# K and G with 512-column products and a transposed 128-column remainder, with 1/den and the reloads of x moved

## Chip, core and metric

The kernel runs on one core of a Trainium2 chip. The metric is device time in microseconds of one execution; the kernel before took 207.70 us in the median of three runs (207.67 to 207.72). TensorE is PE, its weight loads PEld, VectorE DVE, ScalarE ACT, GpSimd POOL, SyncE SP.

## The reference

x has S = 2048 tokens of D = 640. It is normalised (xn), and a linear attention with 32 heads of 20 channels and a gelu MLP with F = 1536 hidden channels both start from xn; everything is bf16.

```python
xn = _layernorm(x)
# attention
q, k, v = xn @ wqkv                       # split by 32 heads of 20 channels
phi = lambda t: where(t > 0, t + 1, exp(t)) + 1e-6
kv  = einsum("bhsd,bhse->bhde", phi(k), v);  z = sum_s phi(k)
o   = (phi(q) @ kv) / (phi(q) . z + 1e-6)
# MLP
h   = gelu(xn @ w1 + b1)
out = x + o @ wo + h @ w2 + b2
```

## The kernel before

Tokens lie in NT = 16 tiles of 128, or NC = 4 chunks of 512; D is DT = 5 blocks of 128. A small planner records every instruction for each engine in the order of the Python code; an engine runs its list in that order, and the planner adds a semaphore wait where an instruction reads or overwrites what another engine or a DMA handles. So the order of the code is the order of each queue, SP's DMA queue and ACT's (which also issues DMAs) included, and an instruction that waits holds all that is behind it on its engine. PSUM is eight banks of 512 fp32 columns, handed out in a ring by take(n).

The stages, in PE's order:

1. Load and layernorm. xn is kept by token (xn_tm) and transposed (xnT, by PE for three tiles, by 13 DMA transposes on SP for the rest, L261). The MLP's first product fills the same time (h_unit, L391, gelu on ACT, L395).
2. K, L500: for each token tile, 5 contraction blocks times two halves of 320 columns, 160 matmuls into a pair of banks. phi (L488 to L491) turns each pair into PK: an exponential on ACT (L488), a min/add on DVE (L489), a max/add on DVE that reads PSUM (L491). PK lies where x was, by token.
3. G = xn^T phi(K), L525 (g_group): the attention's kv is (Wv^T G) per head, so V is never formed. For each of 5 blocks f of xn's channels, 16 token tiles times two halves of 320 columns, 160 matmuls; ACT copies each result to GTb (L529). Beside it DVE adds the 16 tiles of PK in fp32 into zsum (L534, L537) and splits the sum in two bf16 parts, zhl (L540, L543); zsum and zhl lie in the memory of Msb, which is filled later. POOL reorders the columns of Wq (L519).
4. Q in four chunks, L566 (q_chunk), transposed, 512 columns, with the same phi. After chunk 0 come z_step (L549) and kvt_step (L576): the products Wv x G for eight groups of four heads, in two halves u = 0 and u = 1, masked by DVE (L583) and packed by POOL.
5. The output. PE begins the MLP's second product of token tile 0 (out_mm, L696), then the denominators of all tokens (den_mm, L630) and M = blockdiag(kv) Wo (m_step, L620), in the order j = 0, 1, 4, 2, 3. Each half of M is copied from PSUM to Msb: half 0 by ACT (L602), half 1 by DVE (L605). After the third j, m_step calls den_eps (L636), and after the last one den_rec takes the reciprocal (L640). ACT's queue issues 12 DMAs (spread, three for each chunk) that spread 1/den over the partitions into rsp, and scale_pq (L645) multiplies a chunk of PQ by it.
6. Each output tile takes 12 matmuls of the MLP and 5 of the attention (PQ and Msb) of 512 columns. The last 128 columns of chunks 0 to 2 are made transposed (rem_mm, L707), closed by rem_done (L712) and put back by a DMA transpose on SP. main_done (L720) adds x plus b2 and ACT's queue stores the tile; two slots of out_sb are used in turn. Chunk 3 has 640 columns by tile, and tile 15 ends in three pieces (L775).

After Q, SP reloads x: x_again(c) for the four chunks into the memory of xnT, then the last 128 columns of chunks 0 to 2 as xrem into the memory of PK, then three DMA transposes of xrem to xrT, of which rem_done(c) reads one.

Of the kernel before, what the change touches and what calls it, by code (L numbers as in the profile page):

```python
# [7 lines left out]
P = 128  # L8
# [104 lines left out]
def bass_parallel_sum__linear_attn_block__dense_activation_gelu__prompt_kernel(  # L113
# [4 lines left out]
    NT = S // P  # L118
# [22 lines left out]
    with contextlib.ExitStack() as es:  # L141
# [22 lines left out]
        Msb = Mf[:].rearrange("p (k d) -> p k d", k=DT)  # L164
        zsum = Mf[:, 0:2 * D].bitcast(FP32)
        zhl = Mf[:, 2 * D:4 * D].rearrange("p (a d) -> p a d", a=2)
        b1tmp = sb("b1tmp", [JT, P], BF16)
# [38 lines left out]
        def bank(b, lo=0, hi=512):  # L206
            return ps[:, b * 512 + lo: b * 512 + hi]
# [25 lines left out]
        r_PQ = [[R_("PQ%d_%d" % (c, j)) for j in range(DT)] for c in range(NC)]  # L233
        r_HG = [[R_("HG%d_%d" % (t, j)) for j in range(JT)] for t in range(NT)]
        r_GT = [R_("GT%d" % f) for f in range(DT)]
        r_KVT = [R_("KVT%d" % w) for w in range(2)]
# [257 lines left out]

        for t in range(NT):
            b = take(2)
            fns = []
            for k in range(DT):
                for h in range(2):
                    fns.append(lambda e, k=k, h=h, b=b, t=t: e.matmul(  # L500
                        bank(b + h, 0, HW), xnT[:, k, t * P:(t + 1) * P],
                        Wqkv[:, k, D + h * HW:D + (h + 1) * HW], start=(k == 0), stop=(k == DT - 1)))
            Pl.ins(pe, fns, reads=r_xnT[t] + [r_Wk], writes=B_[b:b + 2])
            phi(pair(b), b, 2, PK[:, t, :], r_PK[t], r_x[t])

# [15 lines left out]

        def g_group(f):
            b = take(2)
            for i, t in enumerate(tord):
                Pl.ins(pe, [(lambda e, t=t, h=h, b=b, f=f, i=i: e.matmul(  # L525
                    bank(b + h, 0, HW), xn_tm[:, t, f * P:(f + 1) * P],
                    PK[:, t, h * HW:(h + 1) * HW], start=(i == 0), stop=(i == NT - 1))) for h in range(2)],
                    reads=r_xn[t] + [r_PK[t]], writes=B_[b:b + 2])
            Pl.ins(s_, lambda e, b=b, f=f: e.activation(halves(GTb[:, f, :]), pair(b), ACT.Copy),  # L529
                   reads=B_[b:b + 2], writes=[r_GT[f]] + r_W1)  # L530

        def z_sums():
            a, c = tord[0], tord[1]
            Pl.ins(v, lambda e: e.tensor_tensor(out=zsum, in0=PK[:, a, :], in1=PK[:, c, :], op=ALU.add),  # L534
                   reads=[r_PK[a], r_PK[c]], writes=[r_zsum])
            for t in tord[2:]:
                Pl.ins(v, lambda e, t=t: e.tensor_tensor(out=zsum, in0=zsum, in1=PK[:, t, :], op=ALU.add),  # L537
                       reads=[r_PK[t], r_zsum], writes=[r_zsum])
            for i in range(DT):
                Pl.ins(v, lambda e, i=i: e.tensor_copy(plain(zhl[:, 0, :], i), parts(zsum, i)),  # L540
                       reads=[r_zsum], writes=[r_zhl])
            for i in range(DT):
                Pl.ins(v, lambda e, i=i: e.tensor_tensor(out=plain(zhl[:, 1, :], i), in0=parts(zsum, i),  # L543
                                                         in1=plain(zhl[:, 0, :], i), op=ALU.subtract),
                       reads=[r_zsum, r_zhl], writes=[r_zhl])
# [13 lines left out]
        for f in range(DT):  # L559
            g_group(f)  # L560

        def q_chunk(c):
# [9 lines left out]
        def kvt_step():  # L572
            for u in range(2):
# [5 lines left out]
                    for w in ws for k in range(DT)],  # L579
                    reads=[r_Wv] + r_GT, writes=[B_[b]])  # L580
                for lo, hi, i in ((0, 4, 0),) if u == 0 else ((0, 3, 0), (3, 4, 1)):
# [17 lines left out]
        def m_copy(j, b, h):  # L599
            cols = slice(h * HW, (h + 1) * HW)  # L600
            if h == 0:
                Pl.ins(s_, lambda e: e.activation(Msb[:, j, cols], bank(b + h, 0, HW), ACT.Copy),  # L602
# [5 lines left out]
        def m_step(js, bs, after):  # L608
            for n, (j, b) in enumerate(zip(js, bs)):
                for h in range(2):  # L610
# [13 lines left out]
                    m_copy(j, b, h)  # L624
                if n == 2:
                    after()
# [30 lines left out]

        def x_again(c):
            w = MW if c < NC - 1 else D
            dma("sync", x_res[:, c * CH:(c + 1) * CH, 0:w],  # L660
                xv[c * CW:(c + 1) * CW, 0:w].rearrange("(t p) d -> p t d", p=P), [r_xr[c]] + (sum(r_xnT, []) if c == 0 else []))

# [10 lines left out]
        q_chunk(3)  # L673
        for c in range(NC):
            x_again(c)
        dma("sync", xrem.rearrange("p (t d) -> p t d", t=NT - CH),
            xv[0:(NT - CH) * P, MW:D].rearrange("(t p) d -> p t d", p=P), [r_xrem] + r_PK)
        for c in range(NC - 1):
            dma_t("sync", xrT[:, c * CW:(c + 1) * CW].rearrange("p (t q) -> p t q", t=CH),
                  xrem[:, c * CW:(c + 1) * CW], [r_xrT[c]], reads=[r_xrem])  # L680
        Pl.ins(v, lambda e: e.tensor_copy(b2c[:], b2t[:]), reads=[r_b2t], writes=[r_b2c])
# [55 lines left out]
        for c in range(NC):  # L737
            spread(c)
        scale_pq(0)
        for t in range(1, CH):  # L740
# [77 lines left out]
```

## Time and profile before

| | |
|---|---|
| median of three runs | 207.70 us |
| profiled execution | 207.16 us, of which the span of instructions is 205.10 us |
| PE busy | 200.5 us, 98% of the span |
| DVE, ACT, POOL busy | 109.4, 71.3, 35.2 us |
| granted PE clock | 1.0 in the whole span |
| stage K (59.6 to 81.35 us) | PE 21.75 us of 21.75 |
| stage G (81.35 to 103.1) | PE 21.73 of 21.75, DVE 17.15 |
| stage Q with z and kvt (103.1 to 126.35) | PE 23.11 of 23.25, DVE 19.23 |
| denominators and M (128.94 to 131.95) | PE 2.85 of 3.01 |

The stages are stretches of the trace, cut where PE goes from one line to the next. A matmul's record shows its start exactly and its end by a model, and successive records overlap: 160 records of 299 ns lie in 21.73 us. So what a matmul costs in a stream is the stretch divided by the count, and not the mean of the records. A few records are missing: where a chain piece says x49 for 50 matmuls, its time is still that of 50. The median of the runs is 0.54 us above the profiled execution.

### The profile page before, as it was taken

The numbers are of one execution on the slowest core, as the hardware profiler recorded it, in microseconds if no ns is written. First come the engines' busy times: TensorE is split into PE (matmuls) and PEld (weight loads), VectorE is DVE, ScalarE is ACT, GpSimd is POOL, SyncE is SP. The second block draws the span as 40 slices with busy tenths as digits, with TensorE's granted clock in tenths as the row PEclk, the third lists the DMA queues.
The fourth block names the chain that finished last, engine by engine and source line by source line (L and its number), as shares of the span: only waits on it lengthen the run. The fifth ranks groups of instructions, "written<-read, shape, count | busy, mean of one in ns | idle before, by whom it ended". The sixth has DMA issues, their size and how long they took to land.

```text
span 205.1 us, 3575 instructions
## 1 busy us (share of the span) xinstructions
PE 200.5 (98%) x1375; PEld 120.1 (59%) x1386; DVE 109.4 (53%) x231; ACT 71.3 (35%) x133; POOL 35.2 (17%) x85
## 2 busy tenths in 40 slices
PE   7899999999999999999999999999999999999995
PEld 3898757544457777777746444544444444447774
DVE  3784388100007888999348889564629323513322
ACT  2788777666676555111153554300000000000000
POOL 3342156700000000999100200000000000000000
PEclk9999999999999999999999999999999999999999
DMA  5968746797940000000000000979935111102011
GB/s 148 350 177 123 212 118 126 84 373 258 371 138 0 0 0 3 0 0 3 0 0 3 2 0 9 341 180 165 180 81 152 38 41 51 54 26 51 32 40 59
DMA packets 31386, 20.46 MB, mean 100 GB/s; under 512 B 16521, under 2 KB 31369, under 8 KB 31369
## 3 DMA queue, kind: packets, MB, share of 16 engines
q1 hardware_dynamic: 27888, 17.08, 30.7%
q10 hardware_dynamic: 3480, 3.15, 6.9%
q8 instruction: 11, 0.18, 0.4%
q14 instruction: 7, 0.05, 0.1%
HBM read 13.11 MB, written 2.62 MB: 77 GB/s over the span
## 4 chain that ended last, share of the span: by engine, by line
PE 95%; DVE 1%; DMA 1%; ACT 1%; issue 1%; DVEq 0%
PE ps L696 30%; PE ps L391 25%; PE ps L525 11%; PE ps L500 11%; PE ps L566 10%; PE ps L707 5%; DMA xPK<-in_A_x_dram 1%; DVE stats L342 1%; ACT Msb L602 1%; PE ps L576 1%; PE ps L630 1%; PE ps L329 0%; DVE xn_tm L364 0%; DVE W L775 0%; PE ps L372 0%
## 5 line engine op out<-in xcount | busy, mean ns | idle before, releaser
L391 PE MATMUL ps<-xnT,W 128*128 128x128 bf16 (+3 forms) x402 | 52.6, 292 | 0.2
L696 PE MATMUL ps<-W,HG 128*128 128x512 bf16 (+3 forms) x249 | 46.4, 338 | 0.3 <-ACT Msb L602 0.2
L391 PEld LDWEIGHTS ps<-xnT,W 128*128 128x128 bf16 x405 | 33.8, 98 | 18.3 <-issue 0.2
L395 ACT ACTIVATE HG<-ps,b1c 128x128 bf16<-128x128 f32 (+3 forms) x81 | 39.1, 515 | 14.4 <-PE ps L391 13.3
L696 PEld LDWEIGHTS ps<-W,HG 128*128 128x128 bf16 x252 | 24.0, 98 | 20.4 <-ACT Msb L602 0.2
L488 ACT ACTIVATE ek<-ps 128x512 bf16<-128x512 f32 (+1 forms) x36 | 23.2, 645 | 20.4 <-PE ps L566 10.3
L489 DVE TENSOR_SCALAR ek<-ek 128x512 bf16<-128x512 bf16 (+1 forms) x36 | 11.0, 305 | 32.4 <-ACT ek L488 31.3
L500 PE MATMUL ps<-Wqkv,xnT 128*128 128x320 bf16 x160 | 21.9, 299 | 0.0
L525 PE MATMUL ps<-xPK,xn_tm 128*128 128x320 bf16 x160 | 21.9, 299 | 0.0
L566 PE MATMUL ps<-xnT,Wqkv 128*128 128x512 bf16 x97 | 21.4, 379 | 0.2
L696 PE MATMUL ps<-Msb,PQ 128*128 128x512 bf16 (+3 forms) x104 | 20.8, 338 | 0.1
L500 PEld LDWEIGHTS ps<-Wqkv,xnT 128*128 128x128 bf16 x160 | 15.7, 98 | 6.2
L525 PEld LDWEIGHTS ps<-xPK,xn_tm 128*128 128x128 bf16 x160 | 15.7, 98 | 6.1
L519 POOL COPY Wqkv<-Wqkv 128x128 bf16<-128x128 bf16 x25 | 15.1, 603 | 22.9 <-PE ps L500 21.4
L342 DVE BATCH_NORM_STATS2 stats<-xPK 128x6 f32<-128x320 bf16 x32 | 14.0, 477 | 9.1 <-DMA xPK<-in_A_x_dram 9.1
L720 DVE TENSOR_TENSOR W<-ps,xnT 128x512 bf16<-128x512 f32 x12 | 8.3, 691 | 18.2 <-PE ps L696 12.6
L566 PEld LDWEIGHTS ps<-xnT,Wqkv 128*128 128x128 bf16 x100 | 9.7, 98 | 11.4
L696 PEld LDWEIGHTS ps<-Msb,PQ 128*128 128x128 bf16 x105 | 10.1, 98 | 8.4
L491 DVE SCALAR_TENSOR_TENSOR PQ<-ps,ek 128x512 bf16<-128x512 f32 x20 | 13.8, 691 | 2.1
L491 DVE SCALAR_TENSOR_TENSOR xPK<-ps,ek 128x640 bf16<-128x640 f32 x16 | 13.2, 824 | 1.7
L537 DVE TENSOR_TENSOR Msb<-Msb,xPK 128x640 f32<-128x640 f32 x14 | 11.6, 825 | 0.5
L352 POOL TENSOR_TENSOR rstd<-aggr,mhalf 128x1 f32<-128x1 f32 x16 | 9.9, 621 | 8.9 <-DVE aggr L350 8.9
(64 smaller groups left out, 98.0 us busy)
## 6 DMA issues: line engine op xcount, KB each, us to landing
Wqkv<-in_A_wqkv_dram SPq DMA_DIRECT2D x3, 800.0 KB, 6.8
W<-in_B_w_dram SPq DMA_DIRECT2D x4, 480.0 KB, 5.9
W<-in_B_w_dram SPq DMA_DIRECT2D x1, 1920.0 KB, 12.7
xnT<-in_A_x_dram SPq DMA_DIRECT2D x3, 512.0 KB, 4.8
xn_tm<-rden ACTq DMA_DIRECT2D x12, 128.0 KB, 4.2
out_dram<-W ACTq DMA_DIRECT2D x12, 128.0 KB, 1.7
xPK<-in_A_x_dram SPq DMA_DIRECT2D x4, 320.0 KB, 5.3
Wo<-in_A_wo_dram SPq DMA_DIRECT2D x8, 160.0 KB, 8.3
```

The source lines that it names most:

```text
L342: Pl.ins(v, lambda e: e.bn_stats(stats[:, s, 6 * h:6 * h + 6], x_in[:, t, h * HW:(h + 1) * HW]), reads=r_x[t], writes=[r_stats[s][h]])
L391: Pl.ins(pe, [(lambda e, k=k: e.matmul(bank(b, 0, w), W1[:, k, jb * P:(jb + 1) * P], xnT[:, k, tok], start=(k == 0), stop=(k == DT - 1))) ...
L395: Pl.ins(s_, lambda e: e.activation(HG[:, jb, tok], bank(b, 0, w), ACT.Gelu_apprx_tanh, bias=b1c[:, jb:jb + 1]), reads=[B_[b], r_b1c], wri ...
L488: Pl.ins(s_, lambda e: e.activation(e2, src, ACT.Exp), reads=br, writes=[r_ek[s]])
L489: Pl.ins(v, lambda e: e.tensor_scalar(et, et, 1.0, 1e-6, ALU.min, ALU.add), reads=[r_ek[s]], writes=[r_ek[s]])
L491: Pl.ins(v, lambda e: e.scalar_tensor_tensor(out=d2, in0=src, scalar=0.0, in1=e2, op0=ALU.max, op1=ALU.add), reads=br + [r_ek[s]], writes= ...
L500: fns.append(lambda e, k=k, h=h, b=b, t=t: e.matmul(bank(b + h, 0, HW), xnT[:, k, t * P:(t + 1) * P], Wqkv[:, k, D + h * HW:D + (h + 1) * ...
L519: Pl.ins(g, lambda e, k=k, i=i: e.tensor_copy(plain(Wqkv[:, k, D:2 * D], i), parts(Wqkv[:, k, 0:D], i)), reads=[r_Wq], writes=[r_Wk, r_WqP])
L525: Pl.ins(pe, [(lambda e, t=t, h=h, b=b, f=f, i=i: e.matmul(bank(b + h, 0, HW), xn_tm[:, t, f * P:(f + 1) * P], PK[:, t, h * HW:(h + 1) * H ...
L537: Pl.ins(v, lambda e, t=t: e.tensor_tensor(out=zsum, in0=zsum, in1=PK[:, t, :], op=ALU.add), reads=[r_PK[t], r_zsum], writes=[r_zsum])
L566: Pl.ins(pe, [(lambda e, k=k, j=j, b=b: e.matmul(bank(b), Wqkv[:, k, D + j * P:D + (j + 1) * P], xnT[:, k, cc], start=(k == 0), stop=(k == ...
L696: Pl.ins(pe, [(lambda e, i=i, x=x, bk=bk: e.matmul(bank(bk, 0, x[1] - x[0]), seq[i][0], seq[i][1][:, x[0]:x[1]], start=(i == 0), stop=(i = ...
```

## The change

K is made of two products in each chunk: columns 0 to 511 by token tile, one bank and five matmuls of N = 512 a tile; columns 512 to 639 transposed, five matmuls with 128 columns of Wk as the stationary operand and 512 tokens of xnT as the moving one. Its phi goes to PKT (in the memory of Msb), and a DMA transpose on SP puts it back into PK's last 128 columns. G likewise: g_group covers columns 0 to 511, and the new g_rem makes the last 128 columns of all five blocks transposed (PK as stationary operand, xn_tm as moving one, 512 and 128 columns in turn); ACT copies them to GrT and a DMA transpose on SP puts them into GTb. z_sums waits for these transposes, and kvt_step's half u = 1 for that of G.

In m_step the copies of half 1 for j = 4, 2, 3 go from DVE to ACT, and den_eps is called after the second j. x_again of chunk 0 stays where it was; those of chunks 1 to 3, xrem and its transposes come after spread in the code, and the first of them waits for the three spread DMAs of chunk 0.

```diff
@@ -163,6 +163,8 @@
         Mf = sb("Msb", [P, DT * D], BF16)
         Msb = Mf[:].rearrange("p (k d) -> p k d", k=DT)
         zsum = Mf[:, 0:2 * D].bitcast(FP32)
+        PKT = Mf[:, 0:NC * CW]
+        GrT = Mf[:, 4 * D:5 * D]
         zhl = Mf[:, 2 * D:4 * D].rearrange("p (a d) -> p a d", a=2)
         b1tmp = sb("b1tmp", [JT, P], BF16)
         b1c = sb("b1c", [P, JT], FP32)
@@ -232,6 +234,9 @@
         r_PK = [R_("PK%d" % t) for t in range(NT)]
         r_PQ = [[R_("PQ%d_%d" % (c, j)) for j in range(DT)] for c in range(NC)]
         r_HG = [[R_("HG%d_%d" % (t, j)) for j in range(JT)] for t in range(NT)]
+        r_PKT = [R_("PKT%d" % c) for c in range(NC)]
+        r_PKr = [R_("PKr%d" % c) for c in range(NC)]
+        r_GrT, r_GTr = R_("GrT"), R_("GTr")
         r_GT = [R_("GT%d" % f) for f in range(DT)]
         r_KVT = [R_("KVT%d" % w) for w in range(2)]
         r_KVP = [R_("KVP%d" % i) for i in range(3)]
@@ -492,16 +497,24 @@
                                                        op0=ALU.max, op1=ALU.add),
                    reads=br + [r_ek[s]], writes=[res_dst] + extra_w)
 
-        for t in range(NT):
-            b = take(2)
-            fns = []
-            for k in range(DT):
-                for h in range(2):
-                    fns.append(lambda e, k=k, h=h, b=b, t=t: e.matmul(
-                        bank(b + h, 0, HW), xnT[:, k, t * P:(t + 1) * P],
-                        Wqkv[:, k, D + h * HW:D + (h + 1) * HW], start=(k == 0), stop=(k == DT - 1)))
-            Pl.ins(pe, fns, reads=r_xnT[t] + [r_Wk], writes=B_[b:b + 2])
-            phi(pair(b), b, 2, PK[:, t, :], r_PK[t], r_x[t])
+        for c in range(NC):
+            ts = range(c * CH, c * CH + CH)
+            cc = slice(c * CW, (c + 1) * CW)
+            for t in ts:
+                b = take(1)
+                Pl.ins(pe, [(lambda e, k=k, b=b, t=t: e.matmul(
+                    bank(b), xnT[:, k, t * P:(t + 1) * P], Wqkv[:, k, D:D + MW],
+                    start=(k == 0), stop=(k == DT - 1))) for k in range(DT)],
+                    reads=r_xnT[t] + [r_Wk], writes=[B_[b]])
+                phi(bank(b), b, 1, PK[:, t, 0:MW], r_PK[t], r_x[t])
+            b = take(1)
+            Pl.ins(pe, [(lambda e, k=k, b=b, cc=cc: e.matmul(
+                bank(b), Wqkv[:, k, D + MW:2 * D], xnT[:, k, cc],
+                start=(k == 0), stop=(k == DT - 1))) for k in range(DT)],
+                reads=sum((r_xnT[t] for t in ts), []) + [r_Wk], writes=[B_[b]])
+            phi(bank(b), b, 1, PKT[:, cc], r_PKT[c], [])
+            dma_t("sync", PK[:, c * CH:(c + 1) * CH, MW:D], PKT[:, cc], [r_PKr[c]] + sum((r_x[t] for t in ts), []),
+                  reads=[r_PKT[c]])
 
         tord = list(range(NT))
         def parts(ap, i):
@@ -520,22 +533,33 @@
                        reads=[r_Wq], writes=[r_Wk, r_WqP])
 
         def g_group(f):
+            b = take(1)
+            for i, t in enumerate(tord):
+                Pl.ins(pe, lambda e, t=t, b=b, f=f, i=i: e.matmul(
+                    bank(b), xn_tm[:, t, f * P:(f + 1) * P], PK[:, t, 0:MW], start=(i == 0), stop=(i == NT - 1)),
+                    reads=r_xn[t] + [r_PK[t]], writes=[B_[b]])
+            Pl.ins(s_, lambda e, b=b, f=f: e.activation(GTb[:, f, 0:MW], bank(b), ACT.Copy),
+                   reads=[B_[b]], writes=[r_GT[f]] + r_W1)
+
+        def g_rem():
             b = take(2)
             for i, t in enumerate(tord):
-                Pl.ins(pe, [(lambda e, t=t, h=h, b=b, f=f, i=i: e.matmul(
-                    bank(b + h, 0, HW), xn_tm[:, t, f * P:(f + 1) * P],
-                    PK[:, t, h * HW:(h + 1) * HW], start=(i == 0), stop=(i == NT - 1))) for h in range(2)],
-                    reads=r_xn[t] + [r_PK[t]], writes=B_[b:b + 2])
-            Pl.ins(s_, lambda e, b=b, f=f: e.activation(halves(GTb[:, f, :]), pair(b), ACT.Copy),
-                   reads=B_[b:b + 2], writes=[r_GT[f]] + r_W1)
+                Pl.ins(pe, [(lambda e, t=t, i=i, bk=bk, lo=lo, hi=hi: e.matmul(
+                    bank(bk, 0, hi - lo), PK[:, t, MW:D], xn_tm[:, t, lo:hi], start=(i == 0), stop=(i == NT - 1)))
+                    for bk, lo, hi in ((b, 0, MW), (b + 1, MW, D))],
+                    reads=r_xn[t] + [r_PKr[t // CH]], writes=B_[b:b + 2])
+            for bk, lo, hi in ((b, 0, MW), (b + 1, MW, D)):
+                Pl.ins(s_, lambda e, bk=bk, lo=lo, hi=hi: e.activation(GrT[:, lo:hi], bank(bk, 0, hi - lo), ACT.Copy),
+                       reads=[B_[bk]], writes=[r_GrT])
+            dma_t("sync", GTb[:, :, MW:D], GrT, [r_GTr] + r_W1, reads=[r_GrT])
 
         def z_sums():
             a, c = tord[0], tord[1]
             Pl.ins(v, lambda e: e.tensor_tensor(out=zsum, in0=PK[:, a, :], in1=PK[:, c, :], op=ALU.add),
-                   reads=[r_PK[a], r_PK[c]], writes=[r_zsum])
+                   reads=[r_PK[a], r_PK[c]] + r_PKr[0:1], writes=[r_zsum] + r_PKT)
             for t in tord[2:]:
                 Pl.ins(v, lambda e, t=t: e.tensor_tensor(out=zsum, in0=zsum, in1=PK[:, t, :], op=ALU.add),
-                       reads=[r_PK[t], r_zsum], writes=[r_zsum])
+                       reads=[r_PK[t], r_PKr[t // CH], r_zsum], writes=[r_zsum])
             for i in range(DT):
                 Pl.ins(v, lambda e, i=i: e.tensor_copy(plain(zhl[:, 0, :], i), parts(zsum, i)),
                        reads=[r_zsum], writes=[r_zhl])
@@ -558,6 +582,7 @@
         z_sums()
         for f in range(DT):
             g_group(f)
+        g_rem()
 
         def q_chunk(c):
             cc = slice(c * CW, (c + 1) * CW)
@@ -577,7 +602,7 @@
                     bank(b, (w % 4) * WD, (w % 4) * WD + WD), Wqkv[:, k, 2 * D + E0[w]:2 * D + E0[w] + P],
                     GTb[:, k, w * WD:(w + 1) * WD], start=(k == 0), stop=(k == DT - 1)))
                     for w in ws for k in range(DT)],
-                    reads=[r_Wv] + r_GT, writes=[B_[b]])
+                    reads=[r_Wv] + r_GT + ([r_GTr] if u else []), writes=[B_[b]])
                 for lo, hi, i in ((0, 4, 0),) if u == 0 else ((0, 3, 0), (3, 4, 1)):
                     n = hi - lo
                     Pl.ins(v, lambda e, b=b, u=u, lo=lo, hi=hi, n=n, i=i: e.tensor_tensor(
@@ -598,7 +623,7 @@
 
         def m_copy(j, b, h):
             cols = slice(h * HW, (h + 1) * HW)
-            if h == 0:
+            if h == 0 or j > 1:
                 Pl.ins(s_, lambda e: e.activation(Msb[:, j, cols], bank(b + h, 0, HW), ACT.Copy),
                        reads=[B_[b + h]], writes=[r_M[j][h]])
             else:
@@ -622,7 +647,7 @@
                                 start=(a == 0), stop=last))
                     Pl.ins(pe, fns, reads=reads, writes=[B_[b + h]])
                     m_copy(j, b, h)
-                if n == 2:
+                if n == 1:
                     after()
 
         def den_mm(b):
@@ -655,10 +680,10 @@
                 dma(s_, rsp[:, c, r, :], src, [r_rsp[c][r]] + (sum(r_xn, []) if c + r == 0 else []),
                     reads=[r_rden])
 
-        def x_again(c):
+        def x_again(c, reads=()):
             w = MW if c < NC - 1 else D
             dma("sync", x_res[:, c * CH:(c + 1) * CH, 0:w],
-                xv[c * CW:(c + 1) * CW, 0:w].rearrange("(t p) d -> p t d", p=P), [r_xr[c]] + (sum(r_xnT, []) if c == 0 else []))
+                xv[c * CW:(c + 1) * CW, 0:w].rearrange("(t p) d -> p t d", p=P), [r_xr[c]] + (sum(r_xnT, []) if c == 0 else []), reads)
 
         def xb(t):
             w = MW if t < NT - CH else D
@@ -671,13 +696,7 @@
         q_chunk(1)
         q_chunk(2)
         q_chunk(3)
-        for c in range(NC):
-            x_again(c)
-        dma("sync", xrem.rearrange("p (t d) -> p t d", t=NT - CH),
-            xv[0:(NT - CH) * P, MW:D].rearrange("(t p) d -> p t d", p=P), [r_xrem] + r_PK)
-        for c in range(NC - 1):
-            dma_t("sync", xrT[:, c * CW:(c + 1) * CW].rearrange("p (t q) -> p t q", t=CH),
-                  xrem[:, c * CW:(c + 1) * CW], [r_xrT[c]], reads=[r_xrem])
+        x_again(0)
         Pl.ins(v, lambda e: e.tensor_copy(b2c[:], b2t[:]), reads=[r_b2t], writes=[r_b2c])
         b0 = take(2)
         bb = [(b0 + i) % 8 for i in range(8)]
@@ -736,6 +755,13 @@
         den_rec()
         for c in range(NC):
             spread(c)
+        for c in range(1, NC):
+            x_again(c, r_rsp[0])
+        dma("sync", xrem.rearrange("p (t d) -> p t d", t=NT - CH),
+            xv[0:(NT - CH) * P, MW:D].rearrange("(t p) d -> p t d", p=P), [r_xrem] + r_PK + r_PKr)
+        for c in range(NC - 1):
+            dma_t("sync", xrT[:, c * CW:(c + 1) * CW].rearrange("p (t q) -> p t q", t=CH),
+                  xrem[:, c * CW:(c + 1) * CW], [r_xrT[c]], reads=[r_xrem])
         scale_pq(0)
         for t in range(1, CH):
             out_mm(t, 0, JT, MAIN, first[t:t + 1])
```

## Prediction

> **What bounds the kernel now.** I read the first part of the page and the shares of the chain that ended last, then the chain in order of time, then PE's waits.
>
> ```profile
> PE 200.5 (98%) x1375; PEld 120.1 (59%) x1386; DVE 109.4 (53%) x231; ACT 71.3 (35%) x133; POOL 35.2 (17%) x85
> ...
> PE 95%; DVE 1%; DMA 1%; ACT 1%; issue 1%; DVEq 0%
> ```
>
> PE bounds the kernel, and the chain is PE's own instructions. The chain in order of time (start, length, engine, line, count) shows that the changed stages have no gap:
>
> ```profile
> 59.61 21.73 PE ps L500 x160
> 81.35 21.73 PE ps L525 x160
> ...
> 126.35 2.59 PE ps L696 x12
> 128.94 1.19 PE ps L630 x20
> 130.13 0.17 PE ps L620 x4
> 130.29 0.02 issue
> 130.32 1.53 ACT Msb L602 x4
> 131.85 0.07 issue
> 131.92 7.72 PE ps L696 x35
> ```
>
> K and G are each 160 matmuls of 320 columns in 21.73 us: 135.8 ns each. Twelve of 512 columns take 2.59 us: 215.8 ns. PE's own waits:
>
> ```profile
> PE ps L313 <- PEq L803: 0.8, 1, 0.8
> PE ps L329 <- DVE xn_tm L364: 0.7, 1, 0.7
> PE ps L696 <- ACT Msb L602: 0.2, 1, 0.2
> ```
>
> Two are at the start; the third, 0.2 us, stands between M (L620) and tile 1 (L696). No other wait of PE is there to be removed. So an edit on DVE, ACT or a DMA queue can gain at most that 0.2 us (0.33 us, if the step is counted from the start of the last M product at 131.46 to 131.92, less 0.13 us of streaming); otherwise only PE's own work counts.
>
> **What the Trainium skill says.** "TensorE: Matmul & The Clock Gate", section "Wait — 56ns, not 53.3ns?", gives N/2.4 GHz plus about 2.5 ns a matmul in a stream at full clock. The trace agrees: 215.8 ns is 213.3 + 2.5, 135.8 is 133.3 + 2.5, and the five transposes of 128 columns (L372) take 0.28 us, 56 ns each. The same page, "Step-by-step: what each phase is for", says that the next weights load while a matmul runs; here PEld is busy 120.1 us beside PE, and streams of 128-column matmuls keep 56 ns though a load's record is 98 ns. "DMA: Bandwidth & Descriptors", section "Queues, rings and completion order", says that each DMA engine takes turns between the queues with work for it: SP's and ACT's transfers slow each other. The trace's spread DMAs show contention: the first lands in 3.2 us, others in over 4.
>
> **K.** Removed: 160 x 135.8 ns = 21.73 us. Added: 16 tiles x 5 of 512 columns and 4 chunks x 5 of 512, 100 x 215.8 ns = 21.58 us. The columns are the same (51,200), so what goes is the fixed part of 60 matmuls: -0.15 us, all on PE's path. phi: DVE's pair for a 512-column bank is 0.288 + 0.691 us and some 0.1 us between them; Q, with the same banks at the same pace, shows DVE keeping up with PE at one per 1.08 us. No stall.
>
> **G.** Removed: 21.73 us. Added: 80 x 215.8 = 17.26, and in g_rem 16 x 215.8 = 3.45 and 16 x 56 = 0.90; sum 21.61 us. -0.12 us. Unseen is a stream that alternates 512 and 128 columns on the same weights: bounds are no loss (the 512 hides the load) and 16 x 42 ns = 0.7 us, if the load's 98 ns were exposed in each 128-column step; I take none, as 128-column streams with a load each keep 56 ns. A gain is excluded, since the columns stream anyway.
>
> **The transposes back, and who waits.** This answer on line 261 has the instruction's own time on SP and the time to landing:
>
> ```profile
> L261 SPq DMA_TRANSPOSE xnT<-xn_tm x13: 1199/1200/2072, 12.4 to 36.6; - x13
> L261 SPq DMA_TRANSPOSE xPK<-xPK x6: 1190/1492/2342, 138.5 to 185.1; - x6
> ...
> DMA to landing us min/median/max: 2.4/2.6/6.1
> ```
>
> Five are added on SP, whose queue is idle from 48 to 126 us. *Those of K*: the last phi of K ends about 1.75 us after K's last product (in Q: exponential 0.6, DVE 0.29 and 0.69, gaps), at 82.9; landing 2.6 later, 85.6. z_sums, behind which DVE's phi of Q is queued, must wait for it, because zsum overwrites PKT. Before:
>
> ```profile
> 83.29 0.81 DVE L534 TENSOR_TENSOR Msb<-xPK 128x640 f32<-128x640 bf16 x1
> ...
> 97.84 1.69 DVE L543 TENSOR_TENSOR Msb<-Msb 128x128 bf16<-128x128 f32 x5
> 104.83 0.29 DVE L489 TENSOR_SCALAR ek<-ek 128x512 bf16<-128x512 bf16 x1 [5.30 <-ACT ek L488]
> ```
>
> z_sums starts 2.3 us later and ends at 101.8 and not 99.5; phi of Q comes at 104.6. The idle 5.3 us cover it; at 6.1 us for the landing it would end at 105.3, and the eight banks (5.4 us of PE for five) would take up that 0.7. Cost nil. *That of G*: g_rem ends at 102.8; ACT copies 512 and 128 columns, about 1.0 us; the transpose lands at 103.9 + 2.6 = 106.5. PE needs it for u = 1: after 25 Q matmuls (5.4), z (0.25) and u = 0 (0.73), at 109.2. Cover 2.7 us; at 6.1 us it would cost 0.8. No other transfer runs in those microseconds, so I take 2.6: nil.
>
> **M and 1/den.** The copy that frees tile 1's bank, half 0 of j = 4, is ACT's third copy in both kernels; ACT's three new copies (0.37 us apart) end by 133.3, long before Msb is read at 142. So the 0.2 us stay. DVE loses three copies of 0.48 us: den_eps follows the second copy (131.34), the reciprocal (3.34) ends at 135.4 and not 136.4. scale_pq(0) ended at 141.92; its last part is needed by PE at 142.06 + 4 x 0.216 = 142.9. That gain of 1 us is slack, not time: nothing on PE waited.
>
> **The reloads.** SP holds x_again(1) until the three spread DMAs of chunk 0 land, about 139.9; then 1.66 MB of x, 0.39 MB of xrem, beside nine spreads of 128 KB: 3.2 MB. Behind these stand the transposes of xrem; the first is read by rem_done(0), and behind that on DVE is scale_pq(2), which PE needs at 168.1.
>
> ```profile
> 154.04 0.74 DVE L712 SCALAR_TENSOR_TENSOR xPK<-ps,b2c,xPK 128x512 bf16<-128x512 f32 x1
> ...
> 157.26 1.62 DVE L645 TENSOR_TENSOR PQ<-PQ,xn_tm 128x1024 bf16<-128x1024 bf16 x3
> ```
>
> At the 188 GB/s of the stretch 131.95 to 147.6, 3.2 MB take 17 us: xrem at 156.9; with the slowest such transpose before (5.2 us) rem_done(0) begins at 162.1 and not 154.0. scale_pq(2) comes 3.2 us after and its first part takes 0.7: 166.0, 2.1 us early. If the DMAs don't slow each other it is earlier. Nil, with a cover of 2.1 us from the bad side. scale_pq(1), needed at 149.9, waits for spreads issued by 140.4, which took 4 to 5 us: cover over 3 us.
>
> **Sum.** -0.15 - 0.12 = -0.26 us before rounding of the terms. The profiled execution would take 206.90 us (span 204.84), the median 207.70 - 0.26 = 207.44.
>
> **Rivals.**
> *No saving.* The fixed part of a matmul could be made up elsewhere, by the alternating stream (up to 0.7, part of it): 207.7. For it: that pattern is unseen. Against: the 56 ns streams.
> *The step after M closes too.* If tile 1's bank were really held by ACT and DVE being busy together, fewer DVE copies could free it: -0.33 more, 207.1. For it: the page's wait on ACT. Against: the same third copy of ACT frees the bank in both.
> *Slower: the transpose of GTb comes late.* Place: kvt's half u = 1. It decides if the landing comes after 109.2, 5.3 us after its issue; at the slowest 6.1 us PE stands 0.8 us: 207.44 + 0.8 = 208.24. For it: transposes have taken that long here. Against: only among other transfers.
> *Slower: the reloads come late.* Place: rem_done(0) on DVE. From a start of 164.3 on, each microsecond is one of PE; at 150 GB/s the 3.2 MB end at 161.2, rem_done(0) starts at 166.4, and 2.1 us are lost: 209.5. For it: everything now runs in one stretch. Against: DVE has idle time there.
>
> **How the numbers follow.** A measurement of this kernel can tell about 0.2% (0.4 us) from no change; the forecast gain is 0.13%. Chances: forecast 0.64, no saving 0.08, the M step too 0.12, late GTb 0.09, late reloads 0.07. So faster by over 0.2% 0.12, within it 0.72, slower 0.16. The range is 207.1 (both gains) to 208.4 (late GTb and a little), which leaves out the late reloads and the tails.
>
> **What would show it.** Right: K in 21.58 and G in 21.61 us without a gap on PE; the first product of u = 1 directly behind u = 0; DVE idle ahead of Q's first phi still above 2 us; the reciprocal 1 us sooner with no change on PE. Wrong: a wait of PE on DVE or a DMA at kvt, at Q's banks, or at tile 4 or 8; or g_rem well over 4.35 us.

## The result, and the profile after

| | before | after |
|---|---|---|
| time, median (range, runs) | 207.69 us (207.64 to 207.87, 6) | 206.80 us (206.56 to 206.88, 6) |
| profiled execution | 207.16 us, span 205.1 | 206.67 us, span 204.9 |
| PE busy, instructions | 200.5 us, 1375 | 200.1 us, 1264 |

The ratio of the times is 0.9954, with a 95% interval of 0.9941 to 0.9967: 0.9 us faster. The forecast was 207.44 and its range began at 207.1, so the gain was over three times as large as foreseen. The profiled execution after the change (206.67, span 204.9) is where the working put it (206.90, span 204.84), except that the time outside its span is 1.74 and not 2.06 us. So what was missed lies mostly in how the profiled execution of *before* stands to its other runs.

First the page of the kernel after, with the busy times and the shares of the chain:

```profile
PE 200.1 (98%) x1264; PEld 108.9 (53%) x1278; DVE 108.4 (53%) x236; ACT 73.3 (36%) x142; POOL 34.1 (17%) x85
...
PE 95%; DVE 1%; DMA 1%; ACT 1%; issue 1%; DVEq 0%
```

PE has 111 instructions fewer on record and is still the bound. Its chain in order of time (start, length, engine, line, count; L505 and L511 are K by tile and transposed, L538 is G, L547 g_rem, L591 Q):

```profile
59.69 4.32 PE ps L505 x20
64.01 1.08 PE ps L511 x5
...
81.28 9.71 PE ps L538 x45
90.99 0.05 issue
91.04 7.50 PE ps L538 x34
98.54 2.17 PE ps L547 x16
100.72 0.05 issue
100.77 2.12 PE ps L547 x15
102.89 5.40 PE ps L591 x25
...
130.13 1.46 ACT Msb L627 x4
131.58 0.14 issue
131.73 7.72 PE ps L715 x35
```

K runs from 59.69 to 81.28, 21.59 us where 21.58 were forecast; G with g_rem to 102.89, 21.61 us where 21.61 were. The stream that alternates 512 and 128 columns takes 4.35 us, without a loss. And PE's waits:

```profile
PE ps L318 <- PEq L829: 0.8, 1, 0.8
PE ps L334 <- DVE xn_tm L369: 0.8, 1, 0.8
PE ps L715 <- ACT Msb L627: 0.2, 1, 0.2
```

They are the three of before. By these two profiles the change gains 0.2 us of span and little else; the timed runs say 0.9. The spans of the other executions resolve this. In 58 runs of before that stood beside the first experiments, the median span is 205.7 us (205.0 to 206.3), and the profiled 205.1 is near the bottom. Taking each run's time less its span gives the time outside it.

| | time | span | time outside the span |
|---|---|---|---|
| before | 207.68 | 205.7 | 1.99 |
| after (again, as e4_full) | 206.77 | 205.05 | 1.72 |

The whole change, run again, is again 0.9 us faster, so this is no chance of one set of runs. About 0.65 us is gone from the span, of which the forecast explains 0.26, and about 0.27 us is gone from outside it. The experiments ask where the other 0.4 us of the span and the 0.27 us come from.

### The profile page after: what moved, and what is told of

It reads as the page before. It is cut to its first block, busy times and chain, and to the rows that moved or that the text cites. A ratio compares the mean times of both kernels' runs of the same rounds, so it can differ in the third digit from the quotient of the medians.

```text
span 204.9 us, 3392 instructions
## 1 busy us (share of the span) xinstructions
PE 200.1 (98%) x1264; PEld 108.9 (53%) x1278; DVE 108.4 (53%) x236; ACT 73.3 (36%) x142; POOL 34.1 (17%) x85
## 4 chain that ended last, share of the span: by engine, by line
PE 95%; DVE 1%; DMA 1%; ACT 1%; issue 1%; DVEq 0%
PE ps L715 30%; PE ps L396 26%; PE ps L591 10%; PE ps L505 8%; PE ps L538 8%; PE ps L726 5%; PE ps L547 2%; PE ps L511 2%; DMA xPK<-in_A_x_dram 1%; DVE stats L347 1%; PE ps L601 1%; ACT Msb L627 1%; PE ps L655 1%; PE ps L334 0%; DVE xn_tm L369 0%
## 5 line engine op out<-in xcount | busy, mean ns | idle before, releaser
L493 ACT ACTIVATE ek<-ps 128x512 bf16<-128x512 f32 x40 | 23.8, 598 | 19.3 <-PE ps L591 10.5
L494 DVE TENSOR_SCALAR ek<-ek 128x512 bf16<-128x512 bf16 x40 | 11.5, 288 | 28.3 <-ACT ek L493 28.3
L591 PE MATMUL ps<-xnT,Wqkv 128*128 128x512 bf16 x98 | 21.6, 379 | 0.1
L505 PE MATMUL ps<-Wqkv,xnT 128*128 128x512 bf16 x80 | 17.9, 379 | 0.0
L532 POOL COPY Wqkv<-Wqkv 128x128 bf16<-128x128 bf16 x25 | 14.0, 559 | 22.8 <-PE ps L511 21.3
L538 PE MATMUL ps<-xPK,xn_tm 128*128 128x512 bf16 x79 | 17.4, 379 | 0.1
L591 PEld LDWEIGHTS ps<-xnT,Wqkv 128*128 128x128 bf16 x100 | 9.7, 98 | 11.4
L505 PEld LDWEIGHTS ps<-Wqkv,xnT 128*128 128x128 bf16 x80 | 7.8, 98 | 9.4
L538 PEld LDWEIGHTS ps<-xPK,xn_tm 128*128 128x128 bf16 x80 | 7.8, 98 | 9.4
L496 DVE SCALAR_TENSOR_TENSOR xPK<-ps,ek 128x512 bf16<-128x512 f32 x16 | 11.1, 692 | 1.7
```

What stands on the lines that cost most here:

```text
L493: Pl.ins(s_, lambda e: e.activation(e2, src, ACT.Exp), reads=br, writes=[r_ek[s]])
L494: Pl.ins(v, lambda e: e.tensor_scalar(et, et, 1.0, 1e-6, ALU.min, ALU.add), reads=[r_ek[s]], writes=[r_ek[s]])
L496: Pl.ins(v, lambda e: e.scalar_tensor_tensor(out=d2, in0=src, scalar=0.0, in1=e2, op0=ALU.max, op1=ALU.add), reads=br + [r_ek[s]], writes= ...
L505: Pl.ins(pe, [(lambda e, k=k, b=b, t=t: e.matmul(bank(b), xnT[:, k, t * P:(t + 1) * P], Wqkv[:, k, D:D + MW], start=(k == 0), stop=(k == D ...
L532: Pl.ins(g, lambda e, k=k, i=i: e.tensor_copy(plain(Wqkv[:, k, D:2 * D], i), parts(Wqkv[:, k, 0:D], i)), reads=[r_Wq], writes=[r_Wk, r_WqP])
L538: Pl.ins(pe, lambda e, t=t, b=b, f=f, i=i: e.matmul(bank(b), xn_tm[:, t, f * P:(f + 1) * P], PK[:, t, 0:MW], start=(i == 0), stop=(i == NT ...
```

## Experiments: the parts

The theory after the result was that K and G give 0.26 us of PE's work, and that the earlier 1/den or the later reloads remove a wait which PE has in most executions of before, but did not have in the profiled one. The rival was that all of the gain comes with K and G.

**e1_kg_only.** K and G changed, M's copies and the reloads as before (the edit is against the kernel after):

```diff
-            if h == 0 or j > 1:
+            if h == 0:
-                if n == 1:
+                if n == 2:
                     after()
```

and the reloads of chunks 1 to 3, of xrem and its transposes back in their place behind Q.

> The products of 512 columns for K and G alone, with the transposes back; m_step, 1/den and the reloads as before. The whole change measured -0.89 us where the trace's PE path shows -0.26. Theory A (the excess of about 0.6 us belongs to K and G: fewer instructions, time outside the span or execution to execution): this gives all of it, 206.8 us, and the time less the span falls from 2.06 to about 1.74 us. Theory B (the excess belongs to the reloads or 1/den): only the 0.26 us of the sum, 207.43 us. Theory C (chance between executions, nothing real): 207.43 too, but then the whole change measured again would be at 207.43.

**e2_m_only.** Only M's copies and den_eps, on the kernel before:

```diff
-            if h == 0:
+            if h == 0 or j > 1:
-                if n == 2:
+                if n == 1:
```

> Only the copies of M on ACT and den_eps after the second j; K, G and the reloads as before. Theory A: 207.69 us, no change within 0.1. Theory B, if 1/den is what pays: about 207.1 us. On PE nothing is expected to move; the reciprocal ends 1 us sooner.

**e3_x_only.** Only the reloads of chunks 1 to 3, xrem and its transposes moved behind spread.

```diff
-        for c in range(NC):
-            x_again(c)
+        x_again(0)
...
         spread()
+        for c in range(1, NC):
+            x_again(c, r_rsp[0])
```

> Only the reloads of chunks 1 to 3, xrem and its transposes moved behind spread; K, G and M as before. Theory A: 207.69 us, no change within 0.1. Theory B, if the reloads' place is what pays (transfers that disturb an execution beside M and the first spread): about 207.1 us.

**e4_full.** The whole change, again beside these.

> The whole change again, beside the parts on the same chip. Theories A and B: 206.8 us. Theory C: 207.43 us.

**e5_m_x.** e2's and e3's edits together, without K's and G's.

> The copies of M, den_eps and the reloads as in the change, K and G as before. Theory D (executions of the kernel before lose a varying time, 0.45 us on average, because the spread DMAs of chunk 0 land late beside the reloads and PE waits for scale_pq(0); the profiled execution of before happened not to): this takes the wait away, 207.2 us, with spans within 0.4 us of each other where before has 1.3. Theory E (the gain beyond the sum is K's and G's alone): 207.65 us.

| | time (range, runs) | ratio to before | span | outside |
|---|---|---|---|---|
| e1, K and G | 207.24 (206.69–207.88, 21) | 0.9977 (0.9967–0.9987) | 205.5 | 1.74 |
| e2, M and 1/den | 207.46 (207.18–207.79, 22) | 0.9991 (0.9982–0.9999) | 205.3 | 2.10 |
| e3, reloads | 207.28 (206.93–207.67, 22) | 0.9985 (0.9975–0.9994) | 205.3 | 1.955 |
| e4, all | 206.77 (206.50–206.93, 6) | 0.9952 (0.9936–0.9968) | 205.05 | 1.72 |
| e5, e2 and e3 | 207.43 (207.11–207.90, 21) | 0.9988 (0.998–0.9996) | 205.3 | 2.10 |

Two edits that touch nothing of PE's work, e2 and e3, each take 0.4 us from the span, and together no more. That is how two remedies for one wait look. The rival falls. K and G take 0.2 us from the span, near the forecast 0.26, and the 0.25 us outside the span comes with them alone. In e2 and e5 the time outside the span is 0.1 us longer than in before, so that they gain only 0.2 us in all, less than was expected of them; why was not found.

The wait itself is in e1's trace. First PE's waits, then the stretch 136 to 145 us (start, length, engine, line, operation, idle time before it and its end), then its chain:

```profile
PE ps L721 <- DVE PQ L670: 0.2, 1, 0.2
PE ps L721 <- ACT Msb L627: 0.2, 1, 0.2
```

```profile
138.13 5.99 SPq L266 DMA_TRANSPOSE xPK<-xPK  x3
...
139.99 0.69 DVE L670 TENSOR_TENSOR PQ<-PQ,xn_tm 128x1024 bf16<-128x1024 bf16 x1 [3.26 <-DMA xn_tm<-rden]
...
141.50 0.69 DVE L670 TENSOR_TENSOR PQ<-PQ,xn_tm 128x1024 bf16<-128x1024 bf16 x1 [0.82 <-DMA xn_tm<-rden]
...
143.08 0.43 DVE L670 TENSOR_TENSOR PQ<-PQ,xn_tm 128x512 bf16<-128x512 bf16 x1 [0.89 <-DMA xn_tm<-rden]
143.57 1.69 PE L721 MATMUL ps<-Msb,PQ 128*128 128x512 bf16 x7 [0.17 <-DVE PQ L670]
```

```profile
138.08 4.98 DMA xn_tm<-rden
143.06 0.02 issue
143.08 0.44 DVE PQ L670
```

The third spread DMA of chunk 0 is issued at 138.08 and lands 4.98 us later; the last part of scale_pq(0) (L670) starts on its landing, and PE, at tile 0's attention products, waits for it. The three transposes of xrem run on SP from 138.13 on, beside that DMA. In the profiled execution of before the same lines read:

```profile
138.54 6.13 SPq L261 DMA_TRANSPOSE xPK<-xPK  x3
...
139.64 0.69 DVE L645 TENSOR_TENSOR PQ<-PQ,xn_tm 128x1024 bf16<-128x1024 bf16 x1 [3.23 <-DMA xn_tm<-rden]
...
140.79 1.13 DVE L645 TENSOR_TENSOR PQ<-PQ,xn_tm 128x1024 bf16<-128x1024 bf16 x2 [0.45 <-DMA xn_tm<-rden]
```

There the transposes began 0.8 us after the third spread's issue (137.77), which landed in 3.7 us (141.47), and no wait arose. It is a race between two chains, den to 1/den to spread on one side, the reload of xrem to its transposes on the other. Below, e12 and e16 are the kernel before with edits that leave both chains as they were or nearly so; in their traces the third spread is issued within 0.2 us of the time in before, but the transposes begin 0.8 to 0.9 us earlier (137.75 and 137.66), and PE waits. So a few tenths of a microsecond decide it.

## Experiments: the wait

**e6_before_cover.** The kernel before with more of PE's work ahead of the wait: tile 4's 12 MLP products are made before tile 0's attention products. Nothing about DMAs or DVE changes.

```diff
+        out_mm(CH, 0, JT, MAIN, [bb[3]])
...
-                out_mm(t, 0, NS, MAIN, [b])
+                out_mm(t, JT if t == CH else 0, NS, MAIN, [b])
```

> The kernel before, with the twelve MLP products of tile 4 (2.6 us of PE work that exists anyway) moved ahead of the first product that needs scaled PQ; reloads, M and 1/den as before. Theory D: the wait for scale_pq(0) is covered, so the time is that of moving the reloads and 1/den, 207.2 us, with a narrow spread of spans. If the reloads disturb PE in another way, or the spread of before comes from the start of the kernel: 207.65 us with the spread of before.

207.33 us (207.04 to 207.93, 21; before 207.62), ratio 0.9987 (0.9979 to 0.9996), span 205.4. In its trace the third spread lands late again (138.48 to 143.63) and PE does not wait for it. So what the two remedies take away is a wait of PE, and PE can also cover it.

**e17_before_tlate.** The kernel before, with xrem's three transposes alone moved behind spread, waiting for the spread DMAs of chunk 0. The loads of x and xrem stay early.

```diff
-        for c in range(NC - 1):
-            dma_t("sync", xrT[:, ...], xrem[:, ...], [r_xrT[c]], reads=[r_xrem])
...
+        for c in range(NC - 1):
+            dma_t("sync", xrT[:, ...], xrem[:, ...], [r_xrT[c]], reads=[r_xrem] + r_rsp[0])
```

> The kernel before with only the three DMA transposes of xrem moved behind spread and made to wait for chunk 0's three spread DMAs; the loads of x and xrem stay early. In the profiles with PE's wait the transposes are issued at 137.7 to 138.1, beside the second and third spread, which land 4.1 and 5.0 us after their issue; in the first profile of before, where the transposes came at 138.54, they took 3.6 and 3.7. If the transposes are what slows the spreads (theory D''): the wait goes, third landing under 4 us, span 205.3, 207.28 like the run with all reloads moved. If it is the loads of x: 207.65, third landing 5 us.

207.26 us (207.04 to 207.62, 13; before 207.79 beside it), ratio 0.9974 (0.9962 to 0.9986), span 205.4 against 205.8. From its trace:

```profile
139.93 0.69 DVE L645 TENSOR_TENSOR PQ<-PQ,xn_tm 128x1024 bf16<-128x1024 bf16 x1 [3.22 <-DMA xn_tm<-rden]
140.84 1.05 DVE L645 TENSOR_TENSOR PQ<-PQ,xn_tm 128x1024 bf16<-128x1024 bf16 x2 [0.22 <-DMA xn_tm<-rden]
141.53 6.52 SPq L261 DMA_TRANSPOSE xPK<-xPK  x3
```

The third spread, issued at 138.06, lands at 141.44: 3.4 us. So of the reloads it is these three transposes, and not the loads, that slow the spreads.

**e12_before_late.** The opposite direction: den_eps on the kernel before is called after the last j and not after the third.

```diff
-                if n == 2:
+                if n == 4:
```

> The kernel before with den_eps called after the last j of M and not after the third: by before's trace the reciprocal starts at once behind the same copies, so den_eps at 133.1 delays it by 0.7 us. Theory D: PE's wait for scale_pq(0) grows by the same: +0.5 to +0.7 us, 208.3. If that wait isn't there in most executions: 207.7 to 207.8.

207.72 us (207.05 to 208.56, 22; before 207.70), ratio 1.0003 (0.9993 to 1.0013). The expected loss did not come. DVE has the same five copies and one den_eps to do ahead of the reciprocal, in whichever order: it starts at 133.23, against 133.07 in before. So the place of den_eps is worth about 0.1 us here. In the change the reciprocal starts 1.3 us sooner, at 131.8, 0.2 us of it by K and G; by this, nearly all the rest comes from the three copies on ACT, though the two were not run apart. The trace has the wait all the same, 0.4 us, with a third spread of 5.05 us (137.94 to 142.99).

**e13_before_delay.** The kernel before, den_eps computed twice, which puts 0.68 us on DVE ahead of the reciprocal; the same values are written again.

```diff
+        for _ in range(1):
+            den_eps(bb[1])
         den_rec()
```

> The kernel before with den_eps done twice, so that DVE reaches the reciprocal 0.68 us later (what the run with a late den_eps was meant to do, and did not: the same copies stood before the reciprocal either way). Theory D': in most executions of before PE waits about 0.4 us for scale_pq(0), so nearly all of the 0.68 us is paid: span 206.2 to 206.4, 208.2 to 208.35 in all. If before's wait were rare: 207.7 to 207.9.

209.15 us (208.03 to 209.53, 6; before 207.66), ratio 1.0057 (1.0035 to 1.0078). 0.68 us of delay cost 1.5 us, where 0.5 to 0.7 were expected:

```profile
140.82 0.69 DVE L645 TENSOR_TENSOR PQ<-PQ,xn_tm 128x1024 bf16<-128x1024 bf16 x1 [3.52 <-DMA xn_tm<-rden]
...
143.79 1.03 DVE L645 TENSOR_TENSOR PQ<-PQ,xn_tm 128x1024 bf16<-128x1024 bf16 x2 [2.27 <-DMA xn_tm<-rden]
...
144.76 1.46 PE L696 MATMUL ps<-Msb,PQ 128*128 128x512 bf16 x6 [1.94 <-DVE PQ L645]
```

Now the second and third spread lie wholly beside the transposes (from 137.77) and take 5.7 and 5.5 us. So here a delay of the spread is paid twice: once as such, once in a slower landing.

**e14_after_delay** and **e18_after_delay4.** The same on the kernel after, with den_eps computed two and four times more.

```diff
+        for _ in range(2):
+            den_eps(bb[1])
         den_rec()
```

(e18: range(4).)

> The changed kernel with den_eps done five times in all, so that the reciprocal comes 2.7 us later. By the trace of the changed kernel the last part of scale_pq(0) ends about 1.6 us before PE needs it. Theory D': the first 1.6 us are free and the rest is paid, 206.77 + 1.1 = 207.9. If 1/den has nothing to do with the gain: 206.8.

> The changed kernel with den_eps done five times in all, 1/den 2.7 us later, which the earlier run with three (1.36 us later, inside the slack of 1.6) fell short of. Theory D': the part beyond 1.6 us is paid, 206.8 + 1.1 = 207.9. If 1/den isn't near PE's path in the changed kernel: 206.8.

The text for e14 speaks of five computations and 2.7 us; the kernel made three in all, and by its trace the reciprocal came 1.45 us later. It took 206.81 us (206.69 to 207.15, 5), ratio 0.9954 (0.9942 to 0.9965): nothing lost. e18 made five, 2.9 us later by its trace, and took 207.50 us (207.16 to 207.85, 22), 0.7 us more than after, with 0.5 us of PE's wait for scale_pq(0) in its trace. 1.1 us were expected, from a slack of 1.6 us; these runs put it at 2.2 to 2.4 us. So before stands at the edge of this wait, and after has over 2 us of slack on it.

**e11_after_cover** and **e15_kg_cover.** e6's cover on the kernel after; and K, G and the cover, with M and the reloads as before (its edit is e1's and e6's together).

> The changed kernel with tile 4's twelve MLP products ahead of the first product that needs scaled PQ. Theory D: the change has taken the wait away already, so nothing is gained: 206.77 within 0.1. If some of the wait is left in its slower executions: 206.65.

> K and G as in the change, M, 1/den and reloads as before, and tile 4's MLP products ahead of the first product that needs scaled PQ. Theory D': this cover is worth as much as the second half of the change, 206.8 to 206.9 against 207.24 without it and 206.77 for the whole change. If the second half pays by something other than that wait: 207.2.

e11 took 206.84 us (206.5 to 207.11, 8), ratio 0.9965 (0.9952 to 0.9977): where the wait is gone, the cover brings nothing. e15 took 206.78 us (206.59 to 207.18, 5), ratio 0.9953 (0.994 to 0.9965), span 205.0: K, G and this cover make the whole gain. None of these beats the change by more than the runs scatter.

**All the traces together.** Count PE's time from the first matmul of K to the start of the last five matmuls of the kernel (tile 15's last piece). First before, then e1:

```profile
59.45 1.11 PE L500 MATMUL ps<-Wqkv,xnT 128*128 128x320 bf16 x7
...
202.39 0.44 PE L696 MATMUL ps<-Msb,PQ 128*128 128x128 bf16 x5
```

```profile
60.03 0.59 PE L505 MATMUL ps<-Wqkv,xnT 128*128 128x512 bf16 x2
...
203.04 0.44 PE L721 MATMUL ps<-Msb,PQ 128*128 128x128 bf16 x5
```

| K and G | no wait for scale_pq(0) | with the wait |
|---|---|---|
| of before | 142.93 to 142.94: before, e2, e3, e5, e6, e17 | 143.27 (e16), 143.48 (e12), 144.82 (e13) |
| of the change | 142.67: after, e4, e11, e14, e15 | 143.01 (e1), 143.30 (e18) |

Without the wait the stretch is the same to 0.01 us in every trace. The edit of K and G is worth 0.27 us of it, and the wait costs 0.34 us and more (the list of waits shows less, since it counts idle time only and the ends of matmuls are modelled). What else varies in the span is its start: K's first matmul comes at 59.3 to 60.2 us in these traces. Of the seven traces of kernels that have no remedy for the wait (before, e1, e7, e8, e12, e13, e16), six show it; that of before is the seventh.

## Experiments: K and G apart, and the time outside the span

**e7_k_only.** K of the change, with g_group of before (640 columns, so it waits for K's transposes), no g_rem.

```diff
+            phi(bank(b), b, 1, PKT[:, cc], r_PKT[c], [])
+            dma_t("sync", PK[:, c * CH:(c + 1) * CH, MW:D], PKT[:, cc], ...)
...
-                    reads=r_xn[t] + [r_PK[t]], writes=B_[b:b + 2])
+                    reads=r_xn[t] + [r_PK[t], r_PKr[t // CH]], writes=B_[b:b + 2])
```

> K alone as 512-column products with its transposes back; G, M, 1/den and reloads as before. The sum of the prediction gives -0.15 us: 207.53. If the time outside the span (1.99 us before, 1.72 after) goes with the number of PE instructions (120 of the 216 that the change removes are K's), a further -0.15 and 1.85 us outside the span: 207.38. If it goes with a step of the program's size it is all or nothing: -0.27 or 0.

**e8_g_only.** K of before, with the new g_group and g_rem (which reads PK as K of before writes it).

```diff
         for f in range(DT):
             g_group(f)
+        g_rem()
```

> G alone as 512-column products with g_rem and its transpose back; K, M, 1/den and reloads as before. The sum of the prediction gives -0.12 us: 207.57. With the time outside the span in proportion to PE instructions a further -0.12: 207.45.

e7 took 208.56 us (208.19 to 208.86, 5), ratio 1.0044 (1.003 to 1.0058): slower. PE's waits and the start of G in its trace:

```profile
PE ps L538 <- DMA xPK<-Msb: 1.1, 1, 1.1
PE ps L709 <- DVE PQ L658: 0.8, 1, 0.8
```

```profile
85.57 2.61 PE L538 MATMUL ps<-xPK,xn_tm 128*128 128x320 bf16 x18 [1.07 <-DMA xPK<-Msb]
```

The first block of G reaches token tile 12 before the last transpose of PKT has landed. In the change g_rem stands last and reads the transposed columns from 98.54 on, 13 us after the last of them landed, so the two halves of the edit need each other: g_rem hides K's transposes. e8 took 207.90 us (206.89 to 208.65, 14), ratio 1.0015 (1.0002 to 1.0028), 0.3 us above the upper end of what was expected; its trace has the wait for scale_pq(0), and its spans run from 204.9 to 206.6. Why this kernel is slower than before was not found.

All kernels with K's edit have 1.71 to 1.76 us outside the span (median of the runs), all others 1.92 to 2.10. It is not one value per kernel, though: of the 58 runs of before, eight have 1.67 to 1.77 us, as with K's edit, and the rest 1.88 to 2.11. Three kernels ask which property of K's edit does it.

**e9_after_pe.** The kernel after, with 108 matmuls of one column on PE, so that PE has about as many instructions as before (their result is not used).

```diff
+        filler(108, 1)
```

> The changed kernel with 108 matmuls of one column, of constants, between Q's chunks 1 and 2, so that PE's instructions are as many as before. They cost about 25 ns each on PE, 2.7 us of span. If the time outside the span goes with PE's instructions it returns from 1.72 to 2.0 us; if not, it stays at 1.72.

**e10_after_pool.** The kernel after, with 216 memsets of one column on POOL (of a tile that nothing reads).

```diff
+        for i in range(216):
+            Pl.ins(g, lambda e, i=i: e.memset(spare[:, i:i + 1], 0.0))
```

> The changed kernel with 216 one-column memsets on POOL while it is otherwise idle (about 0.1 us each, beside PE). PE's path is untouched. If the time outside the span goes with the program's whole number of instructions it returns from 1.72 to 2.0 us, 207.05 in all; if it goes with PE's instructions or something else, 206.77.

**e16_before_sp4.** The kernel before, with four DMA transposes on SP in stage K whose result nothing reads.

```diff
+        for c in range(NC):
+            dma_t("sync", spareT[c][:]..., b2bc[:, 0:CW], [r_sp[c]], reads=[r_b2, r_PK[c * CH + CH - 1]])
```

> The kernel before with four DMA transposes of b2's copy into spare tiles on SP during K; nothing waits for them. Every kernel with the change's K has 1.72 to 1.76 us outside the span, those without 1.94 to 2.10. If the four transposes on SP's queue do it, this kernel has 1.74 us; if not, 1.97. The span stays as before, 205.7.

| | time (range, runs) | ratio to before | span | outside |
|---|---|---|---|---|
| e7 | 208.56 | 1.0044 | 206.8 | 1.76 |
| e8 | 207.90 | 1.0015 | 205.95 | 1.965 |
| e9 | 209.51 (209.34–211.05, 6) | 1.0113 (1.0086–1.014) | 207.8 | 1.715 |
| e10 | 211.76 (211.57–212.0, 5) | 1.0202 (1.0185–1.022) | 210.0 | 1.76 |
| e16 | 207.54 (207.19–208.02, 14) | 0.9993 (0.9984–1.0002) | 205.7 | 1.925 |

e9's 2.7 us are PE's time for the 108 products, and e10's 5 us, which were not expected, lie in the span too (see the last section); the time outside the span stays at 1.7 in both. So it is not the number of PE's instructions, nor, by e10, that of all engines, nor, by e16's median, four more transposes on SP, though five of its 14 runs have 1.70 to 1.79 us; by e8 it is not G. What in K's edit does it stays open.

The traces hold a lead that no run here tests. In the kernel before one more 8 KB packet moves after the last instruction, on q14, which the page lists as an instruction queue (the stretch 205.2 to 209 us):

```profile
q14 instruction: 1, 0.01, 0.9%
```

It starts 1.8 us after the last instruction in before, e3, e6, e8, e12, e13 and e17, whose profiled executions have 1.88 to 2.05 us outside the span. In the ten traces with K's edit the last such packet starts 9 to 18 us before the end, and 1.72 to 1.75 us lie outside. How early it comes goes with the number of DVE's instructions on record (231 or 232 in the first group, 236 to 240 in the second); K's edit adds eight, and neither e9, e10 nor e16 changes it. The trace of e16 has no such packet near the end, and 1.75 us. But those of e2 and e5 (228 instructions on DVE) have none either, and 2.08 and 2.09 us, so this is not the whole of it.

## Why the prediction was wrong

- **K and G: right.** -0.15 and -0.12 us were forecast; the stages take 21.59 and 21.61 us, without the wait the traces differ by 0.27 us, and in the timed runs e1's span is 0.2 us below that of before. Neither the alternating stream nor a transpose cost anything: GTb's landed at 106.43 (forecast 106.5; needed at 109), z_sums started at 85.60 (85.6), and DVE was idle for 3.24 us ahead of Q's first phi.
- **The reloads' slack: right.** xrem landed at 153.48, inside the bad-side 156.9 (its transfers are 3.3 MB, 1.7 of them x, and not 3.2, which moves that by 0.4 us); rem_done(0) began at 156.63 (bad side 162.1), scale_pq(2) at 159.86, well before 168.1. The reciprocal came 1.3 us sooner, 0.2 us of it from K and G, so the forecast 1 us is there; the 0.2 us behind M stayed.
- **The step that failed** is "No other wait of PE is there to be removed", and with it, in the part on M and 1/den, "That gain of 1 us is slack, not time: nothing on PE waited". Both hold for the profiled execution and not for the kernel. There the last part of scale_pq(0) had 1 us of slack (141.92 against 142.9); in the traces in which xrem's transposes start with the third spread (e1, e8, e12, e16) it has none, and PE loses 0.3 to 0.5 us. The profile of before itself does not show the wait; that most of its executions pay it follows from four edits of different kinds (e2, e3, e6, e17), each of which lowers its median span by 0.3 to 0.4 us. This is -0.4 us.
- **The sum.** It set the profiled 207.16 against the median 207.70, treated the difference of 0.54 us as a constant, and carried it over. The page showed that the profiled execution was faster than every timed run (207.67 to 207.72); that was the sign that something in it was absent which the others had. Part of those 0.54 us was the wait that the change removes.
- **The time outside the span** was taken to stay at 2.06 us. It fell by about 0.27; the prediction named no reason why it should stay or move, and its cause was not found.
- **A rule used on one side only.** "DMA: Bandwidth & Descriptors", section "Queues, rings and completion order", with its engines that take turns between queues, from the Trainium skill was applied to the reloads as a danger of the change. The same slowing was there in the kernel before, where SP's transposes already lay near ACT's spreads: chunk 0's third spread lands 3.3 to 3.7 us after its issue where the transposes do not run beside it or start well after it, and 4.9 to 5.5 us where they run beside it. The prediction read the spreads of before as "the first lands in 3.2 us, others in over 4"; those of chunk 0 took 3.2, 3.6 and 3.7 us, and the fourth, issued as the transposes began, 4.8. Looked at one by one they pointed at the transposes.
- **The rivals.** None was the cause. The one that closes the step after M named another wait; "no saving" and both slower ones are excluded by the trace.

The sum as measured: -0.26 (K and G) - 0.4 (the wait) - 0.27 (outside the span) = -0.93 us, against -0.9 measured.

## What to carry to other kernels

Compare the profiled execution with the timed median before you build on it: if it is faster than all of them, a wait that most executions have can be missing from the trace, and the places to look for it are those with slack of a microsecond or less behind a DMA. Where a DMA has little slack, transposes on another queue that nobody needs yet can make it late, as here; put them behind it. When a product's last columns are made transposed and put back by a DMA, let the consumer of those columns run last.

## What else the runs showed

**A burst of small POOL instructions held up one DVE instruction to its end.** From e10's trace, the groups and then the stretch:

```profile
L698 POOL MEMSET spare<- 128x1 bf16 x216 | 7.2, 101 | 0.0
```

```profile
114.54 6.95 DVE L495 TENSOR_SCALAR ek<-ek 128x512 bf16<-128x512 bf16 x1
```

A TENSOR_SCALAR that takes 0.28 us elsewhere took 6.95 us, until the last of the memsets (114.16 to 121.34), and PE then stood for 1.9 us; with the waits that followed, the stretch from K on was 4.9 us longer than in after. The Trainium skill, "SBUF — State Buffer", section "Who interferes with whom", names one exclusive lock on the port pair that DVE and GpSimd share. The trace agrees that one blocks the other, and DVE did not get in between the memsets of 0.1 us each: it lost the whole burst.

**The start varies too.** The second piece of W1 arrives at about 8 us, and in some executions PE waits for it; in e6's:

```profile
PE ps L391 <- DMA W<-in_B_w_dram: 0.7, 2, 0.5
```

It is 0.5 us in e1, e11 and e15, 0.2 in e2 and e17, and absent in before and after. It is a part of why K starts between 59.3 and 60.2 us, in kernels with and without the change alike.

**A stream of tiny products and the clock.** In e9's profiled execution the 108 products take 2.87 us (115.0 to 117.9), and in the 3 us behind them the granted clock is 0.55, where it is 1.0 in after. Two of e9's six runs, this one and another, have a mean clock of 0.992 and take 210.6 and 211.1 us; the other four have 1.0 and 209.3 to 209.5. Why it happens in some was not tested.
